# Decode attention with two MLPs on one core: four P buffers, another order of the last two head pairs, and an earlier second sum bank

## The chip, the cores and the metric

The kernel runs on one core of one Trainium2 chip. The metric is device time in microseconds (us) of one execution, as the median of several runs. The engines are PE (TensorE: matmuls, with PEld for its weight loads), DVE (VectorE), ACT (ScalarE), POOL (GpSimd) and SP (SyncE). Each engine works through its own instructions strictly in the order in which they stand in the kernel, and they wait for one another by semaphores.

## The reference

Four tokens (one per batch entry) of width 576 are decoded. The result is x + A(LN(x)) + B(LN(x)), where A is attention over the last 2048 positions of a cache, and B a two-stage MLP. Only what the kernel has to move and multiply is shown:

```python
W = min(4096, max(256, Sk // 4))                 # 2048 of 8192
q = (x @ wq).reshape(B, Sq, 32, 128)             # 32 query heads, 16 K/V heads
k = jnp.repeat(k_cache[:, :, Sk - W:, :], 2, axis=1)
v = jnp.repeat(v_cache[:, :, Sk - W:, :], 2, axis=1)
p = softmax(einsum("bhqd,bhkd->bhqk", q, k) * 128 ** -0.5)
A = einsum("bhqk,bhkd->bhqd", p, v).reshape(B, 1, 4096) @ wo
...
B = x1 + gelu(layernorm(x1) @ w3) @ w4           # w3 576x4608, w4 4608x576
out = x + A + B                                  # x1 = x + shifted gelu(LN(x) @ w1) @ w2
```

With one position per batch entry every shift of B's first stage moves in zeros, so that w1 and w2 do not reach the result and the kernel does not read them.

## The kernel before, in words

**Tiling.** The 16 K/V heads are worked on in 8 pairs, `t` = 0 to 7. A pair has one K tile and one V tile of 128 x 128 x 128 bf16 (4 MB each), loaded by POOL with an indirect DMA into a pool of three tiles that K and V share. A K tile is turned in four quarters on DVE (`k_transpose(t, q)`, L281, two `kt` buffers), each followed by eight score matmuls on PE (`k_scores(t, q, sl)`, L395). Quarters 0 and 1 make the score bank S(t,0), quarters 2 and 3 make S(t,1). `k_mask` (L383) opens each bank. The score banks come in turn from a pool of three PSUM banks (`ps_s`).

**Softmax of a pair.** DVE takes the maxima of each bank (`sm_max`, L401 and L404). A small matmul brings them together (`sm_maxT`, mg, L408), DVE makes the negative maximum (`sm_neg`, L414), another small matmul spreads it (`sm_back`, bp, L419), DVE scales it (`sm_bias`, L424), and ACT takes the exponentials with their row sums (`sm_exp`, L431). DVE turns each of the two E tiles with two instructions into a P buffer `pts[u]` (`sm_turn(t, u)`, L440). There is one P buffer for each half u; ACT clears them at the start (`cleared`, L211), since only the blocks on their diagonal are written later. `sm_den` (PE, L444) and `sm_rec` (DVE, L449 and L450) make the reciprocal of the sum.

**P*V and the output projection.** `pv(t, u, lo, hi)` (L459) issues one matmul for each column c from lo to hi; the 32 of a pair (SC = 16 in each half) add up in one bank O(t). `o_scale` (ACT, L464) scales O, `o_turn` (PE, L470) turns it, `o_sum` (DVE, L480) collects it. For every second pair `o_spread` (PE, R, L489), `o_pick` (DVE, L499 and L502) and `o_proj` (PE, L241, 16 matmuls) multiply four heads by their part of wo and add to the sum. In the last part of the kernel, `a` is pair 6, `o` is pair 5 and `hl` is pair 7. So `o_proj(2 * o + 1)`, which the text calls o_proj(11), takes the heads of pairs 4 and 5, and `o_proj(2 * hl + 1)`, called o_proj(15), those of pairs 6 and 7.

**The sum.** The 576 output columns are two halves, `acc_of(0)` and `acc_of(1)`. They begin in two row groups of one PSUM bank. `acc_split` copies the second half to SBUF on ACT (L232), takes a bank of `ps_s` and puts the half into it with an fp32 matmul (L234, two instructions). From there on the halves lie in two banks. At the end 72 matmuls add the MLP's last product with w4 (`mlp_out`, L241, in six pieces of 18, 7, 5, 4, 1 and 1 columns, each loaded by a DMA of its own, L163), DVE and ACT copy the sums (L693, L695) and SP stores them (L696).

**What sets the order.** The order is written out by hand: a loop over t = 0 to 6 works on the scores of pair t, the softmax and P*V of pair t-1 and the output of pair t-2, and the lines from 627 on do the same for the last pairs. Loads are issued on POOL by `free_one()`, behind the last turn of a K tile and the last P*V of a V tile. The call at L646 is the last; the loads of the fourth part of wo and of w4 that it issues take buffers that are free by then, and follow the load of V(7) on POOL, which the second `free_one()` of the loop (L623) issues for t = 6.

Of the kernel before, what the change touches and what calls it, by code (L numbers as in the profile page):

```python
# [22 lines left out]
def kernel(  # L23
# [14 lines left out]
    nc = tc.nc  # L38
    P = 128
# [13 lines left out]
    QD = 32  # L53
    NQD = P // QD
    NC = W * B * 2 // P
    NU = 2
    NSL = 4
    SC = NC // (NU * NSL)
# [130 lines left out]
    def free_one():  # L189
        pos["free"] += 1  # L190
        flush_loads()
# [15 lines left out]
    def cleared(shape, name):  # L207
        t = const.tile(shape, BF16, name=name)
        flat = t[:] if len(shape) == 2 else t[:].rearrange("p a b -> p (a b)")
        flat = flat.bitcast(F32)  # L210
        nc.scalar.activation(out=flat, in_=zero[:].bitcast(F32).to_broadcast(list(flat.shape)), func=ACT.Copy)  # L211
        return t
# [13 lines left out]
    def acc_of(i):  # L226
        return accs[i][i * QD:i * QD + B, 0:CW]

    def acc_split():
        rows = slice(QD, QD + B)  # L230
        half = const.tile([P, CW], F32, name="half")
        nc.scalar.activation(out=half[rows], in_=acc_of(1), func=ACT.Copy)  # L232
        accs[1] = ps_s.tile([P, NW], F32, tag="S", name="acc1")
        nc.tensor.matmul(out=acc_of(1), lhsT=ident_f[rows, rows], rhs=half[rows],  # L234
                         start=True, stop=False, skip_group_check=True)


    def acc_matmuls(terms):
        for lhsT, rhs in terms:
            for i in range(NI):  # L240
                nc.tensor.matmul(out=acc_of(i), lhsT=lhsT, rhs=rhs[:, i * CW:(i + 1) * CW],  # L241
                                 start=False, stop=False, skip_group_check=True)
# [35 lines left out]
    def k_transpose(t, q):  # L278
        src = kv_tiles["K", t][:].bitcast(I32)[:, q * QC:(q + 1) * QC, :].rearrange("p c (ib i) -> p ib c i", i=QD)
        kt = ktp.tile([P, 2, QC, QD], I32, tag="kt")  # L280
        nc.vector.transpose(out=kt[:], in_=src)  # L281
        kts[t, q] = kt
# [3 lines left out]
    for kb in range(NQD):  # L286
        nc.gpsimd.tensor_copy(out=sel[:, :, :, kb, :],
                              in_=ident_bf[:].rearrange("p (ib i e) -> p ib e i", ib=2, e=2))
# [23 lines left out]
    for g in range(2):  # L312
        nc.gpsimd.tensor_copy(out=same_j[:, g * 2 * QD:(g + 1) * 2 * QD].rearrange("p (e s j) -> p e s j", e=2, j=NJ),
                              in_=sel_j[:].unsqueeze(2).to_broadcast([P, 2, NSL, NJ]))
# [41 lines left out]
    for r in range(2):  # L356
        nc.vector.tensor_copy(out=q_bf[:, r],
                              in_=qT_ps[:, r].rearrange("p u (g x) -> p g u x", g=NQD)[:, :, :, 0:B])
    qs_ps = ps_m.tile([P, Hkv, 4, rep, B], F32, tag="m", name="qs_ps")
    for ie in range(4):  # L360
        ib, e = divmod(ie, 2)
        nc.tensor.matmul(out=qs_ps[:, :, ie], lhsT=sel[:, ib, e].rearrange("p k i -> p (k i)"),
                         rhs=q_bf.rearrange("p r g u b -> p (r g u b)"), start=True, stop=True)
    for kb in range(NQD):
        rows = slice(kb * QD, (kb + 1) * QD)
# [11 lines left out]
    O_ps = {}  # L377
# [3 lines left out]
    def k_mask(t, u):  # L381
        S_ps[t, u] = ps_s.tile([P, NW], F32, tag="S", name="S")
        nc.tensor.matmul(out=S_ps[t, u][:].rearrange("p (c k) -> p c k", k=QD), lhsT=ohT[:],  # L383
                         rhs=negbig[:].unsqueeze(1).to_broadcast([B, SC, QD]),
                         start=True, stop=False, skip_group_check=True)

    def k_scores(t, q, sl):
        u, s = q // 2, q % 2 * 2 + sl
        kt = kts[t, q][:].bitcast(BF16)
        if sl:  # L390
            kts.pop((t, q))
        for ie in range(4):
            ib, e = divmod(ie, 2)
            z0 = (t * 4 + ie) * P + ZP - s * NJ
            nc.tensor.matmul(out=S_ps[t, u][:], lhsT=qz[:, z0:z0 + P],  # L395
                             rhs=kt[:, ib, sl * SC:(sl + 1) * SC, e:2 * QD:2].rearrange("p c k -> p (c k)"),
                             start=False, stop=False, skip_group_check=True)

    def sm_max(t, u):
        mx = small.tile([P, 1], F32, tag="mx")  # L400
        nc.vector.reduce_max(out=mx[:], in_=S_ps[t, u][:], axis=AX.X)  # L401
        if u == 0:
            st["dm", t] = small.tile([P, NU, NG], BF16, tag="dm", name="dm")
        nc.vector.tensor_scalar(out=st["dm", t][:, u, :], in0=sel_g[:], scalar1=mx[:, 0:1], scalar2=None, op0=ALU.mult)  # L404

    def sm_maxT(t):
        mg = ps_m.tile([2 * NJ, NU * NG], F32, tag="m", name="mg")
        nc.tensor.matmul(out=mg[:], lhsT=sel_jb[:], rhs=st.pop(("dm", t))[:].rearrange("p u g -> p (u g)"),  # L408
                         start=True, stop=True)
        st["mg", t] = mg  # L410
# [20 lines left out]
        nc.scalar.activation(out=E[t, u][:].rearrange("p c k -> p (c k)"), in_=S_ps.pop((t, u))[:], func=ACT.Exp,  # L431
                             scale=scale, bias=st["bias", t][:, 0:1], accum_out=st["rs", t][:, u:u + 1])

    pts = [cleared([P, SC, 2 * QD], f"pt{u}") for u in range(NU)]

    def sm_turn(t, u):
        e_in = E.pop((t, u))
        for e in range(2):
            rows = slice(e * 2 * QD, (e + 1) * 2 * QD)
            nc.vector.transpose(out=pts[u][rows, :, e * QD:(e + 1) * QD], in_=e_in[rows])  # L440

    def sm_den(t):
        dn = ps_m.tile([P, NU], F32, tag="m", name="dn")
        nc.tensor.matmul(out=dn[:], lhsT=same_j[:], rhs=st.pop(("rs", t))[:], start=True, stop=True)  # L444
        st["dn"] = dn

    def sm_rec(t):
        rd = small.tile([P, 1], F32, tag="rd", bufs=3)
        nc.vector.reduce_sum(out=rd[:], in_=st.pop("dn")[:], axis=AX.X)  # L449
        nc.vector.reciprocal(out=rd[:], in_=rd[:])  # L450
        st["rd", t] = rd

    def pv(t, u, lo, hi):
        if u == 0 and lo == 0:
            O_ps[t] = ps_o.tile([P, NSL, Dh], F32, tag="O", name="O")
        vn = kv_tiles["V", t][:].rearrange("p (u s c) d -> p u s c d", u=NU, s=NSL)
        for c in range(lo, hi):
            rows = slice(c % 2 * 2 * QD, (c % 2 + 1) * 2 * QD)
            nc.tensor.matmul(out=O_ps[t][rows], lhsT=pts[u][:, c, :], rhs=vn[:, u, :, c, :],  # L459
                             start=(u == 0 and c < 2), stop=False, skip_group_check=True)  # L460

    def o_scale(t):
        O_sb[t] = bigp.tile([P, NSL, Dh], F32, tag="big", name="O_sb")
        nc.scalar.activation(out=O_sb[t][:], in_=O_ps.pop(t)[:], func=ACT.Copy, scale=st.pop(("rd", t))[:, 0:1])  # L464

    def o_turn(t):
        oT = ps_m.tile([P, NSL, P], F32, tag="m", name="oT")
        o = O_sb.pop(t)
        for s in range(NSL):
            nc.tensor.transpose(out=oT[:, s, :], in_=o[:, s, :], identity=ident_w[:, s * NJ:s * NJ + P])  # L470
        st["oT", t] = oT

    def o_sum(t):
        oT = st.pop(("oT", t))
        v = oT[:].rearrange("p s (g x) -> p (s g) x", g=2).rearrange("p g (e x) -> p e x g", e=2)[:, :, 0:NJ]
        k = 2 * t % WOQ
        if k == 0:
            st["on"] = small.tile([P, WOH, B], BF16, tag="on", name="on")
        with nc.allow_low_precision("summed in float32"):
            nc.vector.reduce_sum(out=st["on"][:, k * rep:(k + 2) * rep, :].rearrange("p (e r) b -> p e (r b)", e=2),  # L480
                                 in_=v, axis=AX.X)
# [12 lines left out]
    def o_pick(h):  # L494
        if h % WOQ < WOQ - 1:
            return
        R = st.pop("R")
        mk = small.tile([P, WOR, WOH, B], BF16, tag="mk")
        nc.vector.tensor_tensor(out=mk[:], in0=R[:],  # L499
                                in1=own[:].unsqueeze(1).unsqueeze(3).to_broadcast([P, WOR, WOH, B]), op=ALU.mult)  # L500
        with nc.allow_low_precision("one term is not zero"):
            nc.vector.reduce_sum(out=op[:], in_=mk[:].rearrange("p i h b -> p i b h"), axis=AX.X)  # L502

    def o_proj(h):
        if h % WOQ < WOQ - 1:
            return
        acc_matmuls([(op[:, i, :], wo_tiles[h // WOQ][:, i, :]) for i in range(WOR)])
# [51 lines left out]
    for t in range(NPR - 1):  # L559
        a, o = t - 1, t - 2  # L560
# [26 lines left out]
        if a >= 0:  # L587
            sm_turn(a, 0)
# [4 lines left out]
        if a >= 0:  # L593
            sm_turn(a, 1)
# [32 lines left out]
    hl = NPR - 1  # L627
    a, o = hl - 1, hl - 2
# [13 lines left out]
    k_scores(hl, 1, 0)  # L642
    o_turn(o)
    k_scores(hl, 1, 1)
    k_transpose(hl, 3)
    free_one()  # L646
    o_sum(o)
    k_mask(hl, 1)
    k_scores(hl, 2, 0)
    k_scores(hl, 2, 1)  # L650
    sm_max(hl, 0)
    sm_turn(a, 0)
    sm_turn(a, 1)
    k_scores(hl, 3, 0)
    k_scores(hl, 3, 1)
    sm_max(hl, 1)
    sm_maxT(hl)
    sm_neg(hl)
    sm_den(a)
    sm_rec(a)  # L660
    sm_back(hl)
    sm_bias(hl)
    sm_exp(hl, 0)
    sm_exp(hl, 1)
    o_spread(2 * o + 1)
    o_pick(2 * o + 1)
    pv(a, 0, 0, SC)
    pv(a, 1, 0, SC)
    sm_turn(hl, 0)
    sm_turn(hl, 1)  # L670
    o_proj(2 * o + 1)
    o_scale(a)
    acc_split()
    sm_den(hl)
    sm_rec(hl)
    o_turn(a)
    o_sum(a)
    pv(hl, 0, 0, SC)
    pv(hl, 1, 0, SC)
    o_scale(hl)  # L680
    o_turn(hl)
    o_sum(hl)
# [44 lines left out]
```

## Time and profile before

| what | value |
|---|---|
| median of three runs | 213.25 us (213.08 to 213.5) |
| profiled execution, its own time | 213.73 us |
| its span, first to last instruction | 212.0 us |
| mean granted clock of PE | 0.879 |
| PE busy | 143.4 us (68% of the span) |
| DVE busy | 125.0 us (59%) |
| ACT busy | 28.7 us (14%) |
| POOL busy | 31.3 us (15%) |
| DMA | 87.32 MB, mean 412 GB/s |
| chain of waits, by engine | DMA 51%, PE 26%, DVE 8%, issue 7%, POOL 5% |

The profile shows one execution. A line of the timeline or of the chain of waits begins with the start (us from the beginning of the span) and the duration in us; then come the engine, the line of the kernel and the operation, as out<-in by the program's names, and xN is the number of instructions. In the chain, every piece is what the next one waited for, followed back from the last instruction of the kernel; "issue" is time in which an engine waited for nothing that the profile shows. A bracket such as [2.82 <-DVE dm L404] gives the idle time of the engine ahead of that group and what ended it. In the table of stretches, a line holds the stretch, its length, then the busy time and number of instructions of PE, PEld, DVE, ACT and POOL, then PE's granted clock (1.00 is full speed), the share of time that the DMA engines were busy, and GB/s. The durations of matmuls overlap, so the time of a run of matmuls is read from start to start.

### The profile page before, as it was taken

What the parts mean: (1) busy time and instruction counts of PE and PEld (TensorE: products, weight loads), DVE (VectorE), ACT (ScalarE), POOL (GpSimd) and SP (SyncE); (2) the same over time, 40 slices, a digit from 0 to 9 for tenths busy, and PEclk for the clock granted to TensorE, in tenths of its full rate; (3) what the DMA queues carried; (4) which work ended last, traced back from release to release, by engine and by line L of the source; (5) the groups of instructions that cost most, each with busy time, mean ns of one, the idle gap of its engine ahead of it and who ended that gap; (6) DMA issues with size and microseconds to landing.
All of it is one profiled execution on the core that took longest, in us unless ns stands there. A gap on an engine that the chain in (4) does not pass through costs nothing.

```text
span 212.0 us, 2179 instructions
## 1 busy us (share of the span) xinstructions
PE 143.4 (68%) x879; PEld 59.4 (28%) x892; DVE 125.0 (59%) x177; ACT 28.7 (14%) x59; POOL 31.3 (15%) x62
## 2 busy tenths in 40 slices
PE   0248099659289841089996990969489829859874
PEld 0113033223124210024542430333224303333453
DVE  5510579994289500388829954895389468965120
ACT  6302300110111101003010201200111102022100
POOL 4680001003200210000142011001100270100000
PEclk9999859999969965559999998599969966978999
DMA  7999999999999999999999999999999999989960
GB/s 298 396 476 408 433 458 417 402 470 414 433 453 443 427 425 402 423 461 421 427 455 410 433 451 417 421 464 408 433 451 399 445 434 433 458 376 449 402 253 1
DMA packets 4155, 87.32 MB, mean 412 GB/s; under 512 B 488, under 2 KB 496, under 8 KB 1200
## 3 DMA queue, kind: packets, MB, share of 16 engines
q0 software_dynamic: 3840, 82.45, 90.5%
q1 hardware_dynamic: 296, 4.72, 5.3%
q8 instruction: 7, 0.11, 0.2%
q14 instruction: 4, 0.03, 0.0%
q10 hardware_dynamic: 8, 0.00, 0.0%
HBM read 87.17 MB, written 0.00 MB: 411 GB/s over the span
## 4 chain that ended last, share of the span: by engine, by line
DMA 51%; PE 26%; DVE 8%; issue 7%; POOL 5%; ACT 1%; POOLq 0%; DVEq 0%
DMA kn<-in_A_k_cache_dram,row 26%; DMA vn<-in_A_v_cache_dram,row 24%; PE S L395 9%; PE O L459 9%; DVE kt L281 3%; PE acc L241 3%; PE g_ps L522 2%; POOL kn L125 1%; DVE pt L440 1%; DMA first<-in_A_x_dram 1%; PE oT L470 1%; PE gT_ps L535 1%; DVE mx L401 1%; POOL first L326 1%; POOL wo_sb L147 1%
## 5 line engine op out<-in xcount | busy, mean ns | idle before, releaser
L395 PE MATMUL S<-kt,qz 128*128 128x512 bf16 x243 | 75.9, 436 | 37.5 <-DVE kt L281 35.8
L281 DVE STREAM_TRANSPOSE kt<-kn 128x2048 int32<-128x2048 int32 x32 | 73.7, 2306 | 46.6 <-DMA kn<-in_A_k_cache_dram,row 44.1
L395 PEld LDWEIGHTS <-qz 128*128 128x128 bf16 x256 | 23.4, 104 | 73.6 <-issue 57.1
L459 PE MATMUL O<-vn,pt 128*64 128x512 bf16 x256 | 34.2, 399 | 3.8 <-DMA vn<-in_A_v_cache_dram,row 3.5
L440 DVE STREAM_TRANSPOSE pt<-E 64x512 bf16<-64x512 bf16 x32 | 22.1, 690 | 3.2 <-PE O L459 3.0
L125 POOL DMA_INDIRECT vn<-in_A_v_cache_dram,row x8 | 7.7, 957 | 95.4 <-DVE kt L281 91.6
L431 ACT ACTIVATE E<-S,bias 128x512 bf16<-128x512 f32 x16 | 10.9, 683 | 80.1 <-DVE bias L424 80.1
L459 PEld LDWEIGHTS <-pt 128*64 128x64 bf16 x256 | 13.3, 113 | 20.0 <-issue 10.7
L464 ACT ACTIVATE O_sb<-O,rd 128x512 f32<-128x512 f32 x8 | 5.5, 687 | 61.0 <-PE O L459 61.0
L125 POOL DMA_INDIRECT kn<-in_A_k_cache_dram,row x8 | 7.9, 988 | 37.9 <-DVE kt L281 18.8
L401 DVE TENSOR_REDUCE mx<-S 128x1 f32<-128x512 f32 x16 | 10.6, 665 | 0.1
L522 PE MATMUL g_ps<-w_sb,ln2T 128*32 128x512 bf16 (+1 forms) x50 | 5.8, 567 | 3.8 <-DMA w_sb<-in_B_w_dram 3.8
L383 PE MATMUL S<-negbig,ohT 4*128 4x512 bf16 x16 | 6.4, 398 | 0.2 <-ACT E L431 0.2
L470 PE MATMUL oT<-ident_w,O_sb 128*128 128x128 f32 x32 | 4.9, 275 | 0.8 <-ACT O_sb L464 0.8
L480 DVE TENSOR_REDUCE on<-oT 128x16 bf16<-128x128 f32 x8 | 2.3, 287 | 5.0 <-PE oT L470 4.7
L241 PE MATMUL acc<-wo_sb,op 128*4 128x288 bf16 x64 | 4.6, 286 | 1.0 <-DVE op L502 1.0
L470 PEld LDWEIGHTS oT<-ident_w,O_sb 128*128 128x128 f32 x32 | 3.9, 142 | 2.6 <-ACT O_sb L464 1.3
L241 PE MATMUL acc<-w_sb,gT 128*4 128x288 bf16 x72 | 4.6, 286 | 0.0
L163 POOL DMA_DIRECT2D w_sb<-in_B_w_dram x6 | 3.2, 581 | 7.9 <-DMA vn<-in_A_v_cache_dram,row 7.9
L266 PE MATMUL tp<-ident_bf,first 4*128 4x4 bf16 x8 | 0.6, 173 | 5.5 <-DVE first L253 5.5
L404 DVE TENSOR_SCALAR dm<-sel_g,mx 128x8 bf16<-128x8 bf16 x16 | 3.9, 242 | 0.6
L444 PEld LDWEIGHTS dn<-rs,same_j 128*128 128x128 f32 x16 | 2.8, 188 | 4.4 <-issue 3.4
(100 smaller groups left out, 79.0 us busy)
## 6 DMA issues: line engine op xcount, KB each, us to landing
wo_sb<-in_A_wo_dram POOLq DMA_DIRECT2D x4, 1152.0 KB, 23.1
w_sb<-in_B_w_dram POOLq DMA_DIRECT2D x1, 4608.0 KB, 28.6
wq_sb<-in_A_wq_dram SPq DMA_DIRECT2D x1, 4096.0 KB, 14.0
w_sb<-in_B_w_dram POOLq DMA_DIRECT2D x1, 2592.0 KB, 29.0
w_sb<-in_B_w_dram POOLq DMA_DIRECT2D x2, 576.0 KB, 31.1
w_sb<-in_B_w_dram POOLq DMA_DIRECT2D x1, 1008.0 KB, 30.9
w_sb<-in_B_w_dram POOLq DMA_DIRECT2D x1, 720.0 KB, 32.1
wq_sb<-in_A_wq_dram SPq DMA_DIRECT2D x1, 512.0 KB, 3.5
```

Of the source, the lines that this page charges most:

```text
L125: nc.gpsimd.indirect_dma_start(tl[:].rearrange("p c d -> p (c d)"), None, k_rows if kind == "K" else v_rows, bass.IndirectOffsetOnAxis(ap= ...
L241: nc.tensor.matmul(out=acc_of(i), lhsT=lhsT, rhs=rhs[:, i * CW:(i + 1) * CW], start=False, stop=False, skip_group_check=True)
L281: nc.vector.transpose(out=kt[:], in_=src)
L383: nc.tensor.matmul(out=S_ps[t, u][:].rearrange("p (c k) -> p c k", k=QD), lhsT=ohT[:], rhs=negbig[:].unsqueeze(1).to_broadcast([B, SC, QD] ...
L395: nc.tensor.matmul(out=S_ps[t, u][:], lhsT=qz[:, z0:z0 + P], rhs=kt[:, ib, sl * SC:(sl + 1) * SC, e:2 * QD:2].rearrange("p c k -> p (c k)" ...
L401: nc.vector.reduce_max(out=mx[:], in_=S_ps[t, u][:], axis=AX.X)
L431: nc.scalar.activation(out=E[t, u][:].rearrange("p c k -> p (c k)"), in_=S_ps.pop((t, u))[:], func=ACT.Exp, scale=scale, bias=st["bias", t ...
L440: nc.vector.transpose(out=pts[u][rows, :, e * QD:(e + 1) * QD], in_=e_in[rows])
L459: nc.tensor.matmul(out=O_ps[t][rows], lhsT=pts[u][:, c, :], rhs=vn[:, u, :, c, :], start=(u == 0 and c < 2), stop=False, skip_group_check= ...
L464: nc.scalar.activation(out=O_sb[t][:], in_=O_ps.pop(t)[:], func=ACT.Copy, scale=st.pop(("rd", t))[:, 0:1])
L470: nc.tensor.transpose(out=oT[:, s, :], in_=o[:, s, :], identity=ident_w[:, s * NJ:s * NJ + P])
L522: nc.tensor.matmul(out=g_ps[g * QD:(g + 1) * QD], lhsT=ln2T[:, k, :], rhs=cols[:, :, i0:i0 + n], start=(j == 0), stop=False, skip_group_ch ...
```

## The change

There are four P buffers, not two: pair t uses the two with the parity of t. The other edits are in the hand-written order of the last pairs. `acc_split` goes to the place right behind `k_scores(hl, 1, 1)`. `sm_turn(a, 0)` goes ahead of `k_mask(hl, 1)`. `sm_den(a)` and the P*V matmuls of pair 6 follow the last scores; `sm_maxT`, `sm_neg` and `sm_back` of pair 7 are issued between them. The turns of pair 7 stand ahead of `o_pick(11)`, the P*V of pair 7 ahead of `o_turn(a)`, and o_proj(11) behind it.

```diff
--- before.py
+++ after.py
@@ -431,13 +431,13 @@
         nc.scalar.activation(out=E[t, u][:].rearrange("p c k -> p (c k)"), in_=S_ps.pop((t, u))[:], func=ACT.Exp,
                              scale=scale, bias=st["bias", t][:, 0:1], accum_out=st["rs", t][:, u:u + 1])
 
-    pts = [cleared([P, SC, 2 * QD], f"pt{u}") for u in range(NU)]
+    pts = [cleared([P, SC, 2 * QD], f"pt{u}") for u in range(2 * NU)]
 
     def sm_turn(t, u):
         e_in = E.pop((t, u))
         for e in range(2):
             rows = slice(e * 2 * QD, (e + 1) * 2 * QD)
-            nc.vector.transpose(out=pts[u][rows, :, e * QD:(e + 1) * QD], in_=e_in[rows])
+            nc.vector.transpose(out=pts[t % 2 * NU + u][rows, :, e * QD:(e + 1) * QD], in_=e_in[rows])
 
     def sm_den(t):
         dn = ps_m.tile([P, NU], F32, tag="m", name="dn")
@@ -456,7 +456,7 @@
         vn = kv_tiles["V", t][:].rearrange("p (u s c) d -> p u s c d", u=NU, s=NSL)
         for c in range(lo, hi):
             rows = slice(c % 2 * 2 * QD, (c % 2 + 1) * 2 * QD)
-            nc.tensor.matmul(out=O_ps[t][rows], lhsT=pts[u][:, c, :], rhs=vn[:, u, :, c, :],
+            nc.tensor.matmul(out=O_ps[t][rows], lhsT=pts[t % 2 * NU + u][:, c, :], rhs=vn[:, u, :, c, :],
                              start=(u == 0 and c < 2), stop=False, skip_group_check=True)
 
     def o_scale(t):
@@ -642,41 +642,42 @@
     k_scores(hl, 1, 0)
     o_turn(o)
     k_scores(hl, 1, 1)
+    acc_split()
     k_transpose(hl, 3)
     free_one()
     o_sum(o)
+    sm_turn(a, 0)
     k_mask(hl, 1)
     k_scores(hl, 2, 0)
     k_scores(hl, 2, 1)
     sm_max(hl, 0)
-    sm_turn(a, 0)
     sm_turn(a, 1)
     k_scores(hl, 3, 0)
     k_scores(hl, 3, 1)
+    sm_den(a)
+    pv(a, 0, 0, SC)
     sm_max(hl, 1)
+    sm_rec(a)
+    pv(a, 1, 0, SC // 2)
     sm_maxT(hl)
     sm_neg(hl)
-    sm_den(a)
-    sm_rec(a)
+    pv(a, 1, SC // 2, SC)
     sm_back(hl)
     sm_bias(hl)
     sm_exp(hl, 0)
     sm_exp(hl, 1)
     o_spread(2 * o + 1)
-    o_pick(2 * o + 1)
-    pv(a, 0, 0, SC)
-    pv(a, 1, 0, SC)
     sm_turn(hl, 0)
     sm_turn(hl, 1)
-    o_proj(2 * o + 1)
-    o_scale(a)
-    acc_split()
+    o_pick(2 * o + 1)
     sm_den(hl)
     sm_rec(hl)
+    o_scale(a)
+    pv(hl, 0, 0, SC)
+    pv(hl, 1, 0, SC)
     o_turn(a)
     o_sum(a)
-    pv(hl, 0, 0, SC)
-    pv(hl, 1, 0, SC)
+    o_proj(2 * o + 1)
     o_scale(hl)
     o_turn(hl)
     o_sum(hl)
```

## The prediction

> **What bounds the kernel now.** I read the chain of waits first, from the landing of the last K tile (171.33 us) to the end, then the landings of the loads, then the granted clock. Up to 171 us the chain is mostly loads of K and V, and the DMA share is 0.93 to 1.03 in stretches of 5 us from 170 to 200. But for two clears at the start and the names of the P buffers, nothing of the change lies ahead of 180 us, so the tail counts. The chain of waits there (start, us, what):
>
> ```profile
> 180.38 2.31 DVE kt L281
> ...
> 186.52 0.70 DVE mx L401
> 187.22 0.02 issue
> 187.25 0.24 DVE dm L404
> 187.49 0.04 issue
> 187.53 0.17 PE mg L408
> ...
> 188.26 0.35 PE R L489 x8
> 188.61 5.23 PE O L459 x32
> 193.85 1.09 PE acc L241 x16
> ...
> 196.87 3.59 PE O L459 x32
> ...
> 203.11 0.43 DVE op L502
> 203.54 0.04 issue
> 203.59 5.60 PE acc L241 x88
> ```
>
> See that both blocks of 32 P*V matmuls lie on the path, that the first takes 5.23 us and the second 3.59, and that the end is 88 sums: 16 of o_proj(15), 72 of w4. The stretches of the timeline, by engine, show PE without work from 184.64 to 187.53 (idle before mg 2.82 us), while DVE does `sm_turn(a)` and `sm_max`. The granted clock (second number from behind DMA share) explains the 5.23:
>
> ```profile
> 44.98:48.39 3.41, 1.53 (x13) 0.78 (x12) 3.37 (x4) 0.00 (x0) 0.59 (x1) 1.00 0.96 413
> 167.86:171.27 3.41, 1.34 (x10) 0.52 (x10) 0.00 (x0) 0.69 (x1) 2.10 (x4) 1.00 1.04 444
> 171.27:174.68 3.41, 0.89 (x3) 0.33 (x3) 3.22 (x4) 0.00 (x0) 2.08 (x4) 0.53 1.07 461
> 184.92:188.33 3.41, 0.65 (x7) 0.55 (x7) 2.87 (x9) 0.00 (x0) 0.00 (x0) 1.00 0.98 423
> 188.34:191.75 3.41, 3.41 (x24) 1.64 (x25) 0.97 (x4) 1.45 (x4) 0.00 (x0) 0.53 0.96 408
> ```
>
> The first number after the length is PE's busy time, the third from the end the clock. After a stretch with 0.65 us of work PE gets 0.53 until 191.75. The third bound is the stream of w4. Its last piece in the timeline of POOL (start us, us), and in the issue table (KB, us from issue to landing) below the fourth piece:
>
> ```profile
> 181.27 0.55 POOL L163 DMA_DIRECT2D w_sb<-in_B_w_dram  x1 [7.92 <-DMA vn<-in_A_v_cache_dram,row]
> ```
>
> ```profile
> w_sb<-in_B_w_dram POOLq DMA_DIRECT2D x1, 576.0 KB, 32.9
> w_sb<-in_B_w_dram POOLq DMA_DIRECT2D x1, 144.0 KB, 24.6
> ```
>
> Issue start plus time to landing gives V6 164.73+16.3 = 181.0, V7 169.16+21.5 = 190.7, wo3 170.10+23.3 = 193.4, and the six pieces of w4 (18, 7, 5, 4, 1 and 1 columns) at 199.7, 202.1, 203.8, 205.1, 205.6 and 181.27+24.6 = 205.9. That reckoning fits V6, whose landing at 181.0 frees the waiting POOL at 181.27. Today PE comes to w4 at 203.59+16*0.0636 = 204.6, so no piece is waited for; but the last one lands only 3.3 us before the end of the matmuls (209.19).
>
> **The change, part by part.**
> *Two more P buffers.* Two more clears of 0.62 us on ACT (L211) at 23.9, behind the two at 22.8; ACT is then idle for 17.76 us until the first exp at 41.70, so they cost nothing (1.24 us without that cover). In the loop `sm_turn` never waits for PE: the whole group's wait is 3.0 us in two pieces, 2.70 at 192.23 and 0.30 at 193.96, both in the tail. A layout moved by 4 KB a partition shows in no row; I take 0, bounds -0.2 to +0.2 us (half the spread of the three runs, 0.42).
> *acc_split early.* ACT's copy (0.40) comes after exp(6,1) at 179.43 into an idle ACT. The bank it takes is that of S(6,0), read by 178.7; S(7,1) then takes S(6,1)'s, read by 179.4, before it is needed. PE gets 0.64 us (L234 x2) after `k_scores(7,1)` at 180.35. `k_transpose(7,3)`, which waits for that last score, is ahead of it and keeps 180.38. The mask and the 8 scores of q=2 end near 183.3 instead of 182.6, those of q=3 at 185.25 instead of 184.7. DVE needs them only at 186.6: hidden. No DMA is in it.
> *sm_turn(a,0) ahead of sm_max.* DVE's queue holds the same instructions from 182.69 on: o_sum 0.18, four transposes 2.86, two sm_max (0.61+0.23 and 0.69+0.23). dm is ready at 187.5 as before; `pt(6,0)` at 184.3, `pt(6,1)` at 186.6.
> *P*V of the second-last pair.* sm_den follows the scores: 185.25+0.33 = 185.6. PV, half 0: 16*0.122 = 1.95 (8 take 0.98 at full clock in the loop's rows), to 187.5. PE has no gap, so the clock stays 1.0. The next 8 need pt(6,1) (186.6, ready) and run to 188.5. mg is queued behind them: 188.5 instead of 187.53, **1.0 us late**. sm_rec(6) and then sm_neg on DVE (0.38 from mg's start to nm, as before) end at 188.9; bp waits behind the last 8 PV, to 189.63, and ends at 189.75. Bias, then exp(7,0) at 190.05 instead of 188.56: **1.5 us late**. That is the new cost.
> *What it buys.* exp(7,0) with its sum read ends at 190.8. Its transposes no longer wait for PV: 190.8 to 192.2 (1.42) instead of 192.23 to 193.65; the second pair 192.2 to 193.65 instead of 193.96 to 195.38. On PE: R (0.35) to 190.1, idle, sm_den(7) at 191.55 to 191.9, then PV(7) at 192.25: 32*0.112 to 0.122 = 3.6 to 3.9, so to **195.9 to 196.1** instead of 200.46. V7 has been there since 190.7. o_pick(11) lies on DVE from 193.65 to 194.5, sm_rec(7) to 194.85, o_scale(6) on ACT 191.5 to 192.2: all in time.
> *o_turn(6) and o_proj(11) behind the PV.* o_turn 0.50, o_proj 1.09: PE until 197.55, while ACT does o_scale(7) (0.70) to 196.65. So they cost 0.9 us of the path. Then the old end: o_turn(7) 0.67, o_sum 0.30 and gap, R 0.36, mk 0.43, op 0.43 with 0.04 gaps, together 2.36 (201.23 to 203.59): first sum of o_proj(15) at **199.9 instead of 203.59, 3.7 us sooner**.
> *w4, where the gain is cut.* o_proj(15) 16*0.0636 to 200.95. Pieces: 36 matmuls to 203.2 (landed 199.7), 14 to 204.1 (202.1), 10 to 204.75 (203.8), then a wait for the fourth piece at 205.1, 8 to 205.7, 2 and the last 2 behind the landing at 205.9: end near **206.1 to 206.2**. Without the wait it would be 199.9+5.6 = 205.5. fin and the store (209.21 to 212.0) are unchanged. The end moves from 209.19 to 206.15: **3.0 us** off. The issue times of all these loads are older than the first moved instruction, or (the last, 181.27) hang on V6's landing alone, so I leave the landings where they are.
>
> The profiled execution takes 213.73 us with a span of 212.0 (1.73 around it), 0.48 above the median of the runs, 213.25. Its own sum: span 209.0, 210.7 us. Against the median: 213.25 - 3.0 = **210.25**.
>
> [...] In the grid of 3.41 us stretches above, 1.34 us of work or less was followed by half clock, 1.53 was not. The new idle time (190.1 to 192.25, less 0.35 of den) leaves at worst 3.41-1.8 = 1.6 us of work in a stretch, and with the present grid 1.9: just on the good side. [...]
>
> **Rivals.**
> 1. *The clock falls in the new gap.* PV(7) then runs half its 32 matmuls at 0.213 as in the old first block: +1.64 (5.23-3.59). First o_proj sum at 201.55, end 207.15, no wait for w4: gain 2.05, **211.2**. For it: the edge above, and where the grid lies may differ. Against: 1.9 with the grid of this run. Chance 0.15.
> 2. *w4 lands sooner or PE does not wait for it.* Then 199.9 decides: end 205.5, **209.55**. For it: the stream varies. Against: DMA share 0.98 to 1.03 leaves it nothing to gain. 0.10.
> 3. *It does not do what it says.* The waits come back elsewhere: exp is 1.5 us late, and PV(7) must wait for transposes of 1.42 each. To eat all 3.0 us, and the 0.7 hidden under w4, another 3.7 us must be late; I find no row with it. About **213.25**. 0.07.
> 4. *Slower: the softmax of the last pair queued behind a slow PV.* Place: mg and bp behind 24 and 32 PV matmuls. At half clock throughout, PV(6) takes 32*0.213 = 6.8 instead of 3.6, PV(7) the same: 6.4 us on the path; the first o_proj sum at 206.3, end at 211.9, 2.7 later than today: **215.95**. It decides from 3.7 us on, that is 37 of the 64 matmuls at half clock; before has some 16. Against: the clock rises at 178.10 and PE has work until 190.1. 0.06.
>
> **Numbers.** The forecast has 0.62. Range: from rival 2 to rival 1 with 0.05 below and 0.4 above for pieces of late semaphores, 209.5 to 211.6; outside lie rivals 3 and 4 and tails of the rest, some 0.2. A difference of 0.2% (0.43 us) is about what a measurement of this kernel can tell from none. Faster 0.62+0.15+0.10 = 0.87; same 0.06 of rival 3; slower 0.06 and 0.01 of rival 3.
>
> **What would show it.** PE without a gap from 173.8 to 190; clock 1.0 over the first PV block, which takes 3.6 to 3.9 us in two parts with mg between; exp(7,0) near 190.05; the transposes of the last pair waiting for ACT, not PE; first sum of o_proj(15) near 199.9; and PE waiting in L241 for `w_sb` DMA, with the last landing near 205.9 as now. Wrong would be: a first PV block that waits, a clock of 0.5 between 181 and 200, a later w4, or sums that end before 205.5.

## The result, and the profile after

| | before | after |
|---|---|---|
| median | 213.38 us (213.08 to 213.79, 4 runs) | 210.90 us (210.82 to 211.18, 4 runs) |
| span of the profiled execution | 212.0 us | 209.1 us |
| ratio of the times | | 0.9885 (95% interval 0.9865 to 0.9905) |

The change takes 2.5 us off, in the range and with the sign that were forecast, and 0.5 us less than forecast.

The chain of waits of the changed kernel (start, us, what), at the places that the prediction showed of before:

```profile
184.78 0.12 PE dn L444 x2
184.90 2.71 PE O L459 x24
187.61 0.11 PE mg L408
187.71 0.98 PE O L459 x8
188.70 0.12 PE bp L419
...
191.38 5.29 PE O L459 x32
196.68 0.59 PE oT L470 x4
197.26 1.08 PE acc L241 x16
...
200.63 5.74 PE acc L241 x88
```

See that the first block of P*V now stands where PE had nothing to do, and takes 3.69 us in its two parts; mg is as early as before (187.53 there). But the *second* block takes 5.29 us, where 3.59 were measured before. The stretches of the granted clock (length, busy time of PE, PEld, DVE, ACT, POOL, then clock, DMA share, GB/s) tell why:

```profile
187.86:191.27 3.41, 1.62 (x19) 0.88 (x15) 1.57 (x4) 2.03 (x5) 0.00 (x0) 1.00 0.89 373
191.27:194.68 3.41, 3.30 (x16) 1.46 (x18) 2.54 (x7) 0.00 (x0) 0.00 (x0) 0.51 1.07 452
```

The half clock has not gone, it has moved from the first block to the second, behind the new gap between R and the last P*V: PE is idle for 1.49 us ahead of the last `sm_den` and for 0.41 us behind it. And the end stands against w4. Its last piece, in the issue table and POOL's timeline, and then the last two matmuls in PE's timeline:

```profile
w_sb<-in_B_w_dram POOLq DMA_DIRECT2D x1, 144.0 KB, 24.6
```

```profile
181.41 0.55 POOL L163 DMA_DIRECT2D w_sb<-in_B_w_dram  x1 [8.09 <-DMA vn<-in_A_v_cache_dram,row]
...
206.04 0.29 PE L241 MATMUL acc<-w_sb,gT 128*4 128x288 bf16 x2
```

The piece lands at 181.41+24.6 = 206.0, and the last two sums start at 206.04. The 88 sums take 5.74 us, not 5.60: about 0.1 us of waiting. So two limits fall on nearly the same moment, PE's own chain (200.63+5.60 = 206.2) and the stream. Which of them holds the time can't be read from this profile; the experiments separate them.

### The profile page after: what moved, and what is told of

It reads as the page before. It is cut to its first block, busy times and chain, and to the rows that moved or that the text cites. A ratio compares the mean times of both kernels' runs of the same rounds, so it can differ in the third digit from the quotient of the medians.

```text
span 209.1 us, 2179 instructions
## 1 busy us (share of the span) xinstructions
PE 145.9 (70%) x879; PEld 60.6 (29%) x892; DVE 124.8 (60%) x177; ACT 29.7 (14%) x61; POOL 31.4 (15%) x62
## 2 busy tenths in 40 slices
DMA packets 4156, 87.32 MB, mean 418 GB/s; under 512 B 489, under 2 KB 497, under 8 KB 1201
## 4 chain that ended last, share of the span: by engine, by line
DMA 42%; PE 32%; DVE 13%; issue 8%; POOL 3%; ACT 0%; POOLq 0%; DVEq 0%; ACTq 0%
DMA kn<-in_A_k_cache_dram,row 32%; PE S L395 14%; PE O L459 10%; DMA vn<-in_A_v_cache_dram,row 9%; DVE kt L281 8%; PE acc L241 3%; PE g_ps L522 1%; DVE pt L440 1%; PE oT L470 1%; PE gT_ps L535 1%; DVE mx L401 1%; POOL kn L125 0%; PE R L489 0%; PE S L383 0%; POOL rstd L252 0%
## 5 line engine op out<-in xcount | busy, mean ns | idle before, releaser
L459 PE MATMUL O<-vn,pt 128*64 128x512 bf16 x256 | 36.0, 413 | 5.5 <-DVE kt L281 2.4
L522 PE MATMUL g_ps<-w_sb,ln2T 128*32 128x512 bf16 (+1 forms) x50 | 5.2, 489 | 2.9 <-DMA w_sb<-in_B_w_dram 2.9
L339 PE MATMUL q_ps<-wq_sb,xnT 128*32 128x512 bf16 x40 | 4.5, 629 | 0.9 <-DMA wq_sb<-in_A_wq_dram 0.9
L424 DVE TENSOR_SCALAR bias<-bp 128x1 f32<-128x1 f32 x8 | 1.3, 159 | 5.3 <-PE bp L419 5.3
```

What stands on the lines that cost most here:

```text
L459: nc.tensor.matmul(out=O_ps[t][rows], lhsT=pts[t % 2 * NU + u][:, c, :], rhs=vn[:, u, :, c, :], start=(u == 0 and c < 2), stop=False, skip ...
L522: nc.tensor.matmul(out=g_ps[g * QD:(g + 1) * QD], lhsT=ln2T[:, k, :], rhs=cols[:, :, i0:i0 + n], start=(j == 0), stop=False, skip_group_ch ...
```

## The experiments

**Theory 1**: the P buffers are worth nothing; the gain comes from filling PE's gap ahead of the softmax of the last pair, with what that does to the clock, and from the early sum bank; the landing of w4 (theory A where the clock is concerned) cuts it. **Theory 2**: the buffers make the gain, since they take away a wait of 3.0 us. **Theory B**: only the half clock of the second block cut it. **Theory C**: the clock costs nothing, only the order matters. Each kernel was timed beside runs of the kernel before on its own chip; that kernel's median was 214.06 us for the first four, 213.98 for the second four and 213.75 for the last four. The ratios are not quotients of these medians (for e1 that would be 0.985).

### One part of the change at a time

*New order, two buffers* (e1):

```diff
-    pts = [cleared([P, SC, 2 * QD], f"pt{u}") for u in range(2 * NU)]
+    pts = [cleared([P, SC, 2 * QD], f"pt{u}") for u in range(NU)]
...
-  pts[t % 2 * NU + u]
+  pts[u]
```

> The new order of the last pairs with two P buffers in place of four. Theory 1 (order and early sum bank make the gain, the P buffers nothing): in the changed kernel the P*V of pair 6 out of the first buffer ends at 187.6 us and out of the second at 188.7, and the turns of pair 7 begin at 189.9 and 191.3, so nobody would wait for a buffer: 210.9 us, as the changed kernel, within 0.2. Theory 2 (the extra buffers take away the 3.0 us for which the turns waited for PE): most of the gain is gone, 212.5 to 213.4.

Measured: 210.88 us (ratio to before 0.9818, interval 0.9769 to 0.9868). All of the gain is there without the buffers. DVE's wait for PE at the P buffers is gone, and what the last turns wait for is ACT (us in total, times, longest):

```profile
DVE pt L440 <- ACT E L431: 0.9, 1, 0.9
```

*Old order, four buffers* (e2): the same lines of `pts` edited in the kernel before.

> The old order with four P buffers: one part of the change alone. Theory 1: the turns of pair 7 start near 190.0 instead of 192.2 and wait for nobody, but PE comes to the P*V of pair 7 only at 196.9, behind the P*V of pair 6, o_proj and the sum bank: 213.4 us, no change within 0.2. Theory 2: 210.9 to 211.5, the whole gain or most of it.

Measured: 213.58 us (0.9978, 0.9938 to 1.0018), no change that can be told. DVE's timeline shows the turns of the last pair early, and the chain of waits shows what they gain:

```profile
189.26 2.87 DVE L440 STREAM_TRANSPOSE pt<-E 64x512 bf16<-64x512 bf16 x4
```

```profile
196.34 3.59 PE O L459 x32
```

The turns are done by 192.1 and lie for 4 us. A wait of 3.0 us on DVE had cost nothing, because PE came later still. Theory 2 falls with these two.

*Old order, early sum bank* (e3), and *new order, late sum bank* (e4):

```diff
     k_scores(hl, 1, 1)
+    acc_split()
...
     o_scale(a)
-    acc_split()
```

```diff
     k_scores(hl, 1, 1)
-    acc_split()
...
     o_proj(2 * o + 1)
+    acc_split()
     o_scale(hl)
```

> The old order with the second sum bank set up right behind the scores (7,1): one part alone. Theory 1: the chain of waits loses the copy and the two fp32 matmuls between 194.94 and 196.06, 1.1 us, and nothing else moves: 212.3 us, with the mask 0.6 us later but hidden. Theory 2: no change, 213.4.

> The changed kernel, but the second sum bank set up behind o_proj(11), as it was relative to it before. Theory 1: the copy on ACT (0.40) waits for o_proj, the last o_scale is queued behind it, and o_turn(7) begins some 1.2 us later than 198.3; w4 has landed by then: 212.1 us, and the end near 207.5 in the profile. Theory 2: 210.9, since the split would be hidden either way.

Measured: e3 213.90 us (0.9983, 0.9947 to 1.0020), e4 213.59 us (0.9956, 0.9921 to 0.9990). Both missed, each by some 1.5 us on the slow side; 0.7 us of e3's miss is that the kernel before took 214.06 us on this chip, not the 213.4 that the expectation started from. Neither part alone gives more than about 0.4%, where both together gave 1.15%. The chain of each profile does what was expected: in e3 the copy and the two matmuls are gone from it, and in e4 the copy stands in it again, ahead of the last `o_scale` (the two matmuls run beside that). But see the 88 sums at the end of each chain, first e3, then e4, and the stretches of e3 around them:

```profile
202.86 7.24 PE acc L241 x88
```

```profile
198.39 0.40 ACT half L232
...
201.91 7.12 PE acc L241 x88
```

```profile
199.27:202.68 3.41, 1.45 (x18) 0.73 (x12) 1.01 (x3) 0.69 (x1) 0.00 (x0) 1.00 0.99 415
202.68:206.09 3.41, 3.23 (x28) 1.83 (x30) 0.12 (x1) 0.00 (x0) 0.00 (x0) 0.52 0.56 229
```

7.24 and 7.12 us for what takes 5.60 elsewhere: the clock fell once more, behind the small steps of the output (oT, on, R, mk, op), and took back 1.5 to 1.6 us. In the profiled execution of e3 (214.58 us, one of its slower ones) that turned the gain in the chain into a loss. This is read from one profile each; it is tested below.

### Clock and stream

*Extra matmuls in the gap* (e5), *no wait for the last three pieces of w4* (e6), *both* (e7), and the kernel before with the edit of w4 (e8). The first diff is e5's (in `pv`, the bank is then opened only if it is not open yet), the second that of w4:

```diff
     o_spread(2 * o + 1)
+    O_ps[hl] = ps_o.tile([P, NSL, Dh], F32, tag="O", name="O")
+    for _ in range(7):
+        nc.tensor.matmul(out=O_ps[hl][:].rearrange("p s d -> p (s d)"), lhsT=ident_bf[:],
+                         rhs=kv_tiles["V", a][:, 0:4, :].rearrange("p c d -> p (c d)"),
+                         start=True, stop=True, skip_group_check=True)
     sm_turn(hl, 0)
```

```diff
-        for lo, hi in zip(W4_PIECES, W4_PIECES[1:]):
+        for lo, hi in zip(W4_PIECES[:-3], W4_PIECES[1:-2]):
...
-        acc_matmuls([(gT[:, u, :], w4[:, u, :]) for u in range(lo, hi)])
+        acc_matmuls([(gT[:, u, :], w4[:, min(u, NF - 7), :]) for u in range(lo, hi)])
```

The second edit leaves out less than the expectations say. `zip` still gives four pairs, so that only the last two pieces are not loaded (POOL issues four of the six, and 87.03 MB are moved, against 87.32), and the fourth, of 576 KB, still comes. But the sums of the last six columns read column 29, which lies in the third piece, so that nobody waits for any of the three.

> The changed kernel with seven extra 128x512 matmuls on PE in the gap ahead of the last sm_den, whose result is overwritten, so that PE has work in the gap (1.5 us at 0.216 each). Theory A (w4's last landing at 206.0 holds the end): the clock stays 1.0, the P*V of pair 7 takes 3.6 to 3.7 us instead of 5.29, the first sum of o_proj(15) comes near 199.0 instead of 200.63, and PE then waits for w4: 210.9 us, no more than 0.2 less. Theory B (only the clock cut the gain): 209.3 us.

> The changed kernel without the last three pieces of w4 (0.88 MB left out; the matmuls of those six columns take column 29 instead, so the sum is of other data, and the number of matmuls is as before). Theory A, with PE's own chain as late as the stream (200.63 + 88 sums at 0.0636 = 206.2): 210.8 us, 0.0 to 0.3 less than the changed kernel. If the stream alone held the end: 209 or less.

> Both together: the seven extra matmuls and w4 without its last three pieces (the same six columns left out). Theory A: both limits are gone, the first sum of o_proj(15) near 199.0 and the end near 199.0 + 5.6 = 204.6: 209.2 us, 1.6 less than the changed kernel, while neither edit alone gives more than 0.3. Theory B: the same 209.3 as the extra matmuls alone.

> The kernel before without the last three pieces of w4 (six columns left out as above). Theory A: there the last landing at 205.9 lay 3.3 us ahead of the last sum and nobody waited for it: 213.4 us, no change within 0.2. If the stream of w4 already set the end before the change: up to 2 us less.

| run | median, us | range | ratio to before (interval) |
|---|---|---|---|
| e5, extra matmuls | 210.89 | 210.78 to 211.15 | 0.9851 (0.9812 to 0.9890) |
| e6, edit of w4 | 211.37 | 210.50 to 211.71 | 0.9870 (0.9832 to 0.9908) |
| e7, both | 210.02 | 209.86 to 210.26 | 0.9811 (0.9776 to 0.9846) |
| e8, before with the edit of w4 | 214.07 | 212.99 to 214.44 | 0.9999 (0.9973 to 1.0026) |

PE's timeline of e5 shows theory A at work:

```profile
198.86 1.15 PE L241 MATMUL acc<-wo_sb,op 128*4 128x288 bf16 x16 [0.97 <-DVE op L502]
199.97 3.44 PE L241 MATMUL acc<-w_sb,gT 128*4 128x288 bf16 x50
204.14 0.78 PE L241 MATMUL acc<-w_sb,gT 128*4 128x288 bf16 x10 [0.72 <-DMA w_sb<-in_B_w_dram]
205.51 1.02 PE L241 MATMUL acc<-w_sb,gT 128*4 128x288 bf16 x12 [0.59 <-DMA w_sb<-in_B_w_dram]
```

The sums begin 1.8 us earlier than in the changed kernel, and PE then waits 0.72 and 0.59 us for pieces of w4 and ends where it ended. 1.8 us won on PE are worth nothing, so theory B falls. In e6 PE does not wait for the last pieces, but still pays for its half clock, as its chain shows:

```profile
191.75 5.33 PE O L459 x32
...
201.03 5.60 PE acc L241 x88
```

No gain either, and 0.6 us more than the expected 210.8, with runs 1.2 us apart, where the changed kernel's lie within 0.4. Only both together move the end. The 209.2 us expected of e7 were too bold: the third piece lands at 203.9, PE waits 0.71 us for it, and the 22 sums left then end at 205.5:

```profile
203.97 1.51 PE L241 MATMUL acc<-w_sb,gT 128*4 128x288 bf16 x22 [0.71 <-DMA w_sb<-in_B_w_dram]
```

e8, without any change in time, shows that before the change nobody waited for these pieces.

### All four orders with the clock held

Extra matmuls in every gap of the tail that had cost the clock, in the old order and in the new one, each with the late and the early sum bank. In the old order (`fill(out, n)` issues n of the matmuls above; in the new order 7 stand ahead of the last `sm_den` as in e5, 1 and 4 in the last two gaps, and the late bank has two pairs more, around `acc_split`):

```diff
     sm_max(hl, 1)
+    O_ps[a] = ps_o.tile([P, NSL, Dh], F32, tag="O", name="O")
+    fill(O_ps[a], 12)
     sm_maxT(hl)
...
+    fill(spare, 3)
     o_turn(hl)
     o_sum(hl)
+    fill(spare, 1)
     o_spread(2 * hl + 1)
     o_pick(2 * hl + 1)
+    fill(spare, 4)
     o_proj(2 * hl + 1)
```

> The kernel before, with extra 128x512 matmuls on PE whose results are never read: 12 in the gap ahead of the last sm_maxT (184.64 to 187.5 us) and 3, 1 and 4 in the gaps of the last o_turn, o_spread and o_proj. Nothing else is changed. Theory A (the granted clock is a cost of its own in the tail): the clock stays 1.0 from 178 us on, the first block of P*V takes 3.6 us instead of 5.23, the 88 sums never fall to half clock: 212.1 us in the median (1.6 less than the profiled 213.73) and runs closer together than the 212.8 to 214.6 of the kernel before. Theory C (the clock costs nothing, only the order does): 213.9, as before.

> The same extra matmuls with the early sum bank in the old order. Theory A: the early bank takes 1.1 us off the chain, and with the clock up nothing takes that back: 211.0 us, 1.1 less than the old order with extra matmuls alone; still above the landing of w4 (end near 206.5 against 206.1). Theory C: 213.9, as the early bank without extra matmuls. A third case, the early bank is worth nothing by itself: 212.1, as the old order with extra matmuls.

> The new order with the late sum bank, and extra matmuls in its gaps (7 ahead of the last sm_den; 2, 2, 1 and 4 in the gaps from o_proj(11) on). Theory A: without the two stretches of half clock the first sum of o_proj(15) comes near 200.3 instead of 201.91, the 88 sums take 5.6 and end at 205.9, so the landing of w4 at 206 holds the end: 210.9 us, as the changed kernel, though the bank is late. Theory C: 213.6, as the late bank without extra matmuls. If the late bank costs its 1.2 us whatever the clock: 212.1.

> The changed kernel with the same extra matmuls in all gaps of its tail (7 ahead of the last sm_den, 1 and 4 in the last two). Theory A: PE is ready at 204.6, w4 lands at 206: 210.8 us, as the changed kernel. If something besides the landing holds it: 209.3. It is also the candidate for a kernel that does not depend on where the clock falls.

| median, us (ratio to before, interval) | late bank | early bank |
|---|---|---|
| old order, as it is | 213.75 | 213.90 (0.9983, 0.9947 to 1.0020) |
| old order, clock held | 212.15 (0.9945, 0.9925 to 0.9964) | 210.88 (0.9880, 0.9859 to 0.9902) |
| new order, as it is | 213.59 (0.9956, 0.9921 to 0.9990) | 210.90 (0.9885, 0.9865 to 0.9905) |
| new order, clock held | 211.00 (0.9887, 0.9867 to 0.9907) | 210.93 (0.9884, 0.9863 to 0.9906) |

But for the 213.75, the rows "as it is" come from other chips than the rows with the clock held; the ratios are what compares. With the clock held, the early bank takes 1.27 us off the old order's median (1.1 expected), and in the new order the late bank no longer costs anything: both end with the landing of w4 (206.1 with the late bank, where PE's own chain, 200.57+5.60 = 206.2, is as late, and 206.0 with the early one). Theory C falls. The chain of the old order with the clock held:

```profile
188.29 3.57 PE O L459 x32
191.86 1.09 PE acc L241 x16
...
194.89 3.57 PE O L459 x32
...
201.60 5.60 PE acc L241 x88
```

The first block takes 3.57 us in place of 5.23 (the granted clock was 1.00 from 184.92 to 191.75), the sums 5.60. And the old order with early bank and clock held reaches the time of the changed kernel without any of its reordering. No run beats the changed kernel but e7, which leaves work out: three roads end at 210.9. That the last pieces of w4 hold the end is seen in the profile of the new order with early bank and clock held:

```profile
205.23 1.02 PE L241 MATMUL acc<-w_sb,gT 128*4 128x288 bf16 x12 [0.59 <-DMA w_sb<-in_B_w_dram]
```

For the old order it is argued, not seen. Its profiled execution with the early bank was the slowest of its five (211.75 us; the others 210.81 to 210.96), no faster than the profiled one with the late bank, and its sums ran without a wait from 201.58 to 207.18, later than the last landing (206.1). One expectation missed here too: the runs of the old order with the clock held are not closer together (211.75 to 212.85) than those of the kernel before beside them (all but one 213.01 to 214.06). Where the clock rises in the tail, which the extra matmuls do not change, still moves the chain (last section); that this makes the spread of the runs is likely, but not shown.

## Why the prediction was right, point by point

- *Two more P buffers: 0.* Shown by e1 and e2.
- *acc_split early: hidden, 1.1 us off the chain.* Right in the chain, and with the clock held (w_split against w_before) it shows as 1.27 us in the medians. As a step by itself it is worth nothing measurable while the clock can fall at the end (e3).
- *mg 1.0 us late, exp 1.5 us late.* Mis-sized. The scores ended at 184.78 instead of 185.25, and 24 matmuls of P*V took 2.71 us, 0.113 each, where I reckoned 0.122 from groups of eight in the loop. mg came at 187.61, within 0.1 us of before, and exp(7,0) at 189.09, 0.5 us late.
- *PV(7) in 3.6 to 3.9 us.* Failed. The first rival, given a chance of 0.15, happened, with its place and its price: the clock fell behind the new gap, and the block took 5.29 us. A clock of 0.5 between 181 and 200 was also one of the signs named for being wrong. I had taken 1.53 us of work in a stretch as enough to keep the clock, and here 1.62 was not; that one row was a poor guide (last section).
- *First sum of o_proj(15) at 199.9.* Measured 200.63. Of the two errors (0.9 us too late up to the turns, some 1.6 too early behind them) 0.7 us is left; that they worked against each other is luck.
- *The end near 206.15, on the landing of w4.* Right in the number (last landing 206.0 as forecast, 205.9; last pair at 206.04; span 209.1 against 209.0), and half right in the reason. PE was forecast to be ready at 205.5 and to wait; with the half clock it was ready at 206.2, and waited only about 0.1 us. So two limits hold the end, of which the forecast had one: e5 shows that without the half clock the stream still holds it, e6 that without the last pieces the half clock does. That the half clock cost almost nothing is luck: it fell into time that w4 hid.
- *Against the median: 213.25 - 3.0 = 210.25.* The measured 210.90 lies in the range, but nearer to the first rival's 211.2. This is the term that was mis-sized, by 0.5 us. The profiled execution before lay above its median (213.73 against 213.25), and I took that distance over. But the changed kernel's end hangs on w4, so its own time 209.1+1.73 = 210.8 is also its median; the prediction's other sum, 210.7, was the one to give.

## What to carry to other kernels

Read the end of a tail from both sides: the chain of the engines, and the landing of the last loads. Here a gain in the chain counted only down to the landing of w4 near 206.0 us: of the 1.8 us that e5 won on PE nothing was seen. A wait with a large number, such as DVE's 3.0 us for a buffer, is worth nothing if the next in the chain comes later still (e2, 213.58 us, no change that can be told). And when PE's gaps were moved here, the half clock behind them moved too, from the first block of P*V (5.23 us before) to the second (5.29 us after); price each gap of the new order, down to the small steps at the very end, and do not trust an edge that rests on one row.

## What the runs showed of the hardware

In the profiles of before and after the granted clock changes between 1.00 and 0.50 on a grid: the changes lie whole multiples of 3.41 us apart (before: a fall at 171.46, a rise at 178.28, a fall at 188.52, a rise at 191.94; after: 170.87, 177.70, 191.35, 194.77).

Where the changes lie differs from run to run: with the first turn of the last K tile at 171.43 to 171.81 us in every profile, the clock rose again between 177.1 (e5) and 179.8 us (w_split). A later rise went with a later mg: in the four profiles of the old order with the late bank, mg starts at 187.21 (w_before), 187.31 (e2), 187.36 (e8) and 187.53 us (before), with rises at 177.2, 177.4, 177.7 and 178.3.

The clock fell behind windows in which PE was busy for up to about half of the time (1.76 of 3.41 us in e4). The stretches of 3.41 us shown up to here begin some 0.1 to 0.2 us ahead of the grid. Laid exactly between the changes of the clock, they give this (e4, after and before, each with its next window):

```profile
198.23:201.64 3.41, 1.76 (x16) 0.81 (x14) 0.92 (x3) 1.09 (x2) 0.00 (x0) 1.00 1.01 423
201.64:205.06 3.42, 3.15 (x28) 1.73 (x30) 0.22 (x1) 0.00 (x0) 0.00 (x0) 0.50 0.83 342
167.46:170.87 3.41, 1.70 (x11) 0.55 (x10) 0.00 (x0) 0.69 (x1) 1.74 (x3) 1.00 0.98 423
170.87:174.29 3.42, 0.37 (x1) 0.10 (x1) 2.73 (x2) 0.00 (x0) 2.46 (x5) 0.50 0.93 402
45.17:48.58 3.41, 1.59 (x11) 0.83 (x12) 3.37 (x4) 0.00 (x0) 0.78 (x1) 1.00 0.93 404
48.58:51.99 3.41, 3.41 (x24) 1.07 (x22) 1.40 (x5) 0.00 (x0) 1.29 (x3) 1.00 0.98 423
```

The clock fell behind e4's 1.76 us, behind the 1.70 us of the changed kernel, and behind the 1.54 us ahead of its last P*V. It stayed up behind the 1.59 us of before, which is the row (1.53 in its own stretch) that the prediction took as the edge. So the busy time that the profile shows does not tell by itself behind which window the clock fell; what else counted was not shown.
